# Retention followed by a bilinear FFN: slots 8 to 11 as one tile, two pairs of blocks by seven products, and a new order of all steps

## The chip, the cores and the metric

One core of one Trainium2 chip. The metric is device time in microseconds of one execution of the whole kernel. Five engines work side by side, each through its own queue in order: TensorE (PE, with its weight loads shown as PEld), VectorE (DVE), ScalarE (ACT), GpSimd (POOL) and SyncE (SP), which here issues nearly all DMAs. An instruction that waits holds up everything behind it on its engine.

## The reference

```python
# q, k, v: (4, 8, 768, 64); gamma_h = 1 - 2**(-5-h); scale = 1/8
for t in range(768):
    state = gamma * state + outer(k[t], v[t])          # per batch and head
    y[t] = scale * (q[t] @ state)
x = y.transpose(0, 2, 1, 3).reshape(3072, 512)
out = ((x @ w_a) * (x @ w_b)) @ w_out                  # w_a, w_b: 512x1536, w_out: 1536x512
```

Inputs and output are float32. The kernel computes in bfloat16 products with float32 sums.

## The kernel before

**Slots and tiles.** The 3072 tokens are 24 slots of 128, six to a batch. Attention works on slots; the FFN works on tiles of several slots: `TILES = [4, 2, 2, 2, 2, 4, 8]`. Slots 0 to 5 (three pairs, `PAIRS = 3`) come first and have routines of their own (`casts2`, `flip2`, `scores2`, ...), because their transposes are done on TensorE; from slot 6 on `flip` does them by DMA.

**A slot of attention** from slot 6 on: `scaled` multiplies k and q by tables of the decay and casts to bfloat16 into `kqb`; the cast of v goes into `vb`; `flip` transposes `kqb` into `kqT` by a DMA on SP; `update` (U) adds the slot's k, v products to the state and copies the state to SBUF; `scores` (S) gives masked scores `aT` (two products with the mask on VectorE); `inter` (I) and `intra` (N) sum the output in two PSUM banks; `leave` (L), once for two slots, copies the output to the tile `xt` on ScalarE. `turn(new, old)` does U and S of one pair of slots and I, N and L of the pair before it in one go, some 70 small TensorE products without an FFN product between.

**The FFN of a tile.** The width of 1536 is 12 blocks of 128. For a block, `ffn_a` multiplies a weight block with the whole tile (four products over the depth of 512), and ScalarE casts the result to bfloat16 (`asb`); `ffn_g` does the same with the other weights and VectorE multiplies the two into `ht`. A tile of two slots has products of 256 columns, one of four slots 512. PSUM banks of these blocks come from a ring of three (`psff`).

**Seven products for eight.** A 2x2 block product can be done with seven products of sums of blocks. The kernel does this in three places: in `Group` (the output product of two slots: sums `hs` of `ht`, sums T1 to T4 of w_out; steps numbered 1, 7, 2, 6, 5, 3, 4), in `Unit` (the input products of the last tile, slots 16 to 23; sums of weights `ws` and of inputs `XS`), and in `Quad` (two pairs of blocks, 0 with 6 and 1 with 7, of the tile of slots 12 to 15, one object for each weight, sums of inputs `XF`). Results are evicted between the steps: a bank `A` keeps summing and ScalarE takes snapshots of it, which VectorE adds to the banks `B` and `C`.

**The order** of the instructions on every engine is the order of the calls in the program (`seq` pins it). It is written out by hand: for slots 6 to 15 by calls such as these, for slots 12 to 15 and the end by strings (`LACED`, `START`, `END`).

```python
blocks(3, 9, 10)
turn(12, 10)
blocks(3, 10, NFT)
hsums(3, 3, 6, G_)
casts(16)
single(3, Y0, AT0, FF)     # Group of tile 3, with blocks 0 to 2 of tile 4 between its steps
```

Weight sums for the last tiles are made on GpSimd by `weight_pieces`, a few at a time. Loads of a slot follow the `flip` of the slot two before it. `store` issues the finished output rows.

**The start.** SP issues k, q, v of pair 0, of pair 1, then the first weights. For the first six slots k, q and v come with two tokens to a partition: runs of 512 bytes.

```python
f = raw_tile([P, H, 2, D], F32, nm + "f", nm + "f")
s = src[b, :, 2 * u * P : 2 * (u + 1) * P, :].rearrange("h (p two) d -> p h two d", two=2)
seq(nc.sync.dma_start(out=f, in_=s))
```

**Buffers that matter here**: output rows `osb` have six buffers, used in turn, also for the sums `XF`; `asb` five; raw k and q two, each for two slots; `kqT` three, each for two slots; `xt` and `ht` two.

Of the kernel before, what the change touches and what calls it, by code (L numbers as in the profile page):

```python
# [9 lines left out]
F32 = mybir.dt.float32  # L10
# [5 lines left out]
TILES = [4, 2, 2, 2, 2, 4, 8]  # L16
PAIRS = 3


START = ("A1 A2 u0.1 u1.1 A6 T X3 A7 B1 X2 A5 B6 B7 X1 A3 B5 u0.2 u1.2 B2 X4 A4 u0.6 B3 u1.6 B4 u0.5 u1.5 "  # L20
         "u0.7 u2.1 u0.3 u1.7 u2.6 u1.3 u0.4 u2.2 u3.1 u2.5 u1.4 u2.7 u3.6")
END = ("u11.1 u10.5 u10.7 u9.4 u11.6 u10.3 u11.2 S03 a1< u11.5 u11.7 u10.4 b1< u11.3 a1> b1> c1< d1< u11.4 a7 c1> d1> c2 d2 "
       "S02 S01 b7 a2 b2 S04 a6 b6 S13 a5 b5 S12 a3 b3 a4 b4 S11 c7 d7 c6 d6 S14 c5 d5 "
       "c3 c4 d4 d3")
V_LATE = range(12, 20)
LACED = ("X3 X2 m1 m7 m2 a1 b1 a2 b2 m6 X1 a6 b6 a7 b7 F2 X4 m5 a5 b5 K20 G2 a3 b3 a4 b4 V18 "
         "m3 c1 d1 F3 H3 c2 d2 c6 d6 c7 d7 c5 d5 m4 c3 d3 V19 c4 d4 G3")
# [4 lines left out]
def kernel(  # L32
# [78 lines left out]

    def raw_tile(shape, dtype, tag, name):
        return raw.tile(shape, dtype, tag=tag, name=name, bufs=3 if tag == "vf" else 2)
# [3 lines left out]
    def load_slot(t, names="kqv"):  # L117
        b, ci = divmod(t, NCH)
        for nm in names:
            src = {"k": k, "q": q, "v": v}[nm]  # L120
            if nm == "q":
                if t % 2 == 0:
                    load_two(nm, src, b, ci // 2, t)
                continue
            if t % 2 == 0:
                whole[nm] = raw_tile([P, 2, H, D], F32, nm + "f", nm + "f")
            raws[nm, t] = whole[nm][:, t % 2]
            s = src[b, :, ci * P : (ci + 1) * P, :].rearrange("h p d -> p h d")
            seq(nc.sync.dma_start(out=raws[nm, t], in_=s))

    def load_slots(t):
        for u, names in ((t, "kq"), (t + 1, "k"), (t, "v"), (t + 1, "v")):
            load_slot(u, names)
# [8 lines left out]
    def load_pair(u):  # L142
        for nm, src in (("k", k), ("q", q), ("v", v)):
            load_two(nm, src, 0, u, 2 * u)
# [25 lines left out]
    def issue_loads(n):  # L170
        for _ in range(min(n, len(pending))):
            what = pending.pop(0)
            n = int(what[1:])
            if what[0] in "ab":
                load_wide(what[0], n)
            elif what[0] in "kqv":
                load_two(what[0], {"k": k, "q": q, "v": v}[what[0]], 0, n, 2 * n)
            else:
                {"p": load_pair, "s": load_slots, "t": load_slot, "w": load_w, "o": load_o}[what[0]](n)


    kqb = {}
# [11 lines left out]
    tabs = []  # L194

    def tables(pattern, channel):
# [8 lines left out]
        if not tabs:  # L205
            qtab = const.tile([P, NCH, H, 1], F32, name="qtab")
            seq(nc.scalar.activation(qtab[:, :, :, 0], earg, AF.Exp, bias=bq))
            tabs.append(qtab)
        tabs.append(ktab)

    tables([[2 * P, PAIRS], [1, 2], [0, 1]], 2)
    make_identity(nc, ident)
# [4 lines left out]
    for par in range(2):  # L217
        m = const.tile([P, 1, P], BF16, name=f"mask{par}")
        seq(nc.gpsimd.memset(m, 1.0))
        for c in range(2):  # L220
            mc = m[64 * c : 64 * c + 64]
            seq(nc.gpsimd.affine_select(out=mc, in_=mc, compare_op=ALU.is_ge, fill=0.0,
                                        base=-par, pattern=[[0, 1], [1, 2], [2, 64]],
# [5 lines left out]
    def late_tables():  # L229
# [3 lines left out]
        tables([[P, NCH], [0, 1]], 1)  # L233

# [32 lines left out]
    def cast_o(j):  # L267
        cast(nc.gpsimd, wo_bf[:, j * FPO : (j + 1) * FPO, :], wst["o", j])
# [12 lines left out]
    def scaled(eng, t, i):  # L281
        tab = tabs[0] if i else tabs[1 if t < 2 * PAIRS else 2]
# [5 lines left out]
        else:  # L288
            dst = dst.rearrange("p hp r d -> p r hp d")
# [3 lines left out]

    def new_nat(t):
        kqb[t] = nat.tile([P, 2, HP, 2, D], BF16, tag="kqb", name="kqb")
        kb[t], qb[t] = kqb[t][:, 0], kqb[t][:, 1]
        vb[t] = nat.tile([P, H, D], BF16, tag="vb", name="vb")

    def casts(t, between=lambda: None):
        new_nat(t)  # L300
        scaled(nc.gpsimd, t, 0)
        between()
        scaled(nc.gpsimd, t, 1)
        if t not in range(12, 20):
            cast(nc.gpsimd, vb[t], raws["v", t])
        u = t + 2
        if u == 20:
            load_slot(u, "kq")
        flip(t)
        if u == 20:  # L310
            load_slot(u + 1, "k")
            return
        if u == 21:
            load_slot(u - 1, "v")
            load_slot(u, "v")
            load_slot(22, "kq")
            return
        if u in V_LATE:
            if u == 13:
                load_slot(12, "q")  # L320
            elif u == 19:
                load_slot(18, "kq")
            load_slot(u, {12: "k", 18: ""}.get(u, "kq"))
            if u % 2:
                load_slot(u - 1, "v")
                load_slot(u, "v")
        elif u < NSLOT:
            load_slot(u)

    def flip(t):  # L330
        if t % 2 == 0:
# [4 lines left out]

    def late_kq(t):
        for u in (t, t + 1):
            new_nat(u)
            scaled(nc.gpsimd, u, 0)  # L340
            scaled(nc.gpsimd, u, 1)
            flip(u)
        if t == 20:
            load_slot(23, "k")
            load_slot(22, "v")
            load_slot(23, "v")

    def casts_two(t):
        for u in (t, t + 1):
            new_nat(u)  # L350
            scaled(nc.gpsimd, u, 0)
            scaled(nc.gpsimd, u, 1)
            flip(u)
        for u in (t, t + 1):
            cast(nc.gpsimd, vb[u], raws["v", u])
        load_slot(t + 3)
# [9 lines left out]
    def scores(t, where, cuts=2):  # L366
        at = score_banks(where)
# [13 lines left out]
    def update(t, eng):  # L381
        ci = t % NCH
        if ci == NCH - 1:
            return
# [17 lines left out]

    def inter(t):
        if t % NCH == 0:
            return
        for j in range(2):
# [8 lines left out]
    def intra(t):  # L415
        for r in range(2):
# [7 lines left out]
    def leave(t):  # L424
        J, i = where[t]
# [7 lines left out]

    def turn(new, old, eng=nc.scalar):
        if old is not None:
            ys[old // 2] = [psat.tile([P, 2, 2, 2, P // 2], F32, tag=f"y{r}", name="y") for r in range(2)]
        two = new is not None and (new + 1) % NCH < NCH - 1
        if new is not None:
            if two or old is None:
                update(new, eng)  # L440
            cuts = 1 if new == 8 else 2
            scores(new + 1, "y" if old is None else "ff", cuts)
            scores(new, "at", cuts)
        if old is not None:
            inter(old)
            inter(old + 1)
        if two:
            update(new + 1, nc.scalar)
        elif new is not None and old is not None:
            update(new, eng)  # L450
        if old is not None:
            intra(old)
            intra(old + 1)
            leave(old)

# [24 lines left out]

    def scores2(u, par, where="at"):
# [787 lines left out]
```

## Time and profile before

| | |
|---|---|
| median of 3 runs | 218.31 us (218.28 to 218.43) |
| span of the profiled execution | 216.6 us |
| outside the span, to the median | 1.7 us |
| TensorE busy | 210.7 us, 97% |
| GpSimd, VectorE, ScalarE busy | 154.2, 147.5, 104.9 us |
| DMA | 39.68 MB, 183 GB/s over the span |

How to read the views: a row of the timeline has the start and the length in us, the engine, the line of the kernel, the operation, the tile written and the tiles read, the shape, the count, and in brackets the idle time before it with what ended it. Products of TensorE overlap, so the distance of starts, not the length, is what one costs. A row by form has after the bar the busy time in us and the mean ns of one. A row of the windows has start and end, the length, busy time and count of PE, PEld, DVE, ACT and POOL, then the granted clock, the busy share of the DMA engines and GB/s. The lines of the kernel that appear below: L568 and L580 the blocks a and g, L685 the groups' steps, L390 U, L372 S, L410 I, L420 N, L378 the masks, L431 L, L292 the scaled casts of k and q, L251 and L249 casts, L618 sums and products of two tiles.

### The profile page before, as it was taken

What the parts mean: (1) busy time and instruction counts of PE and PEld (TensorE: products, weight loads), DVE (VectorE), ACT (ScalarE), POOL (GpSimd) and SP (SyncE); (2) the same over time, 40 slices, a digit from 0 to 9 for tenths busy, and PEclk for the clock granted to TensorE, in tenths of its full rate; (3) what the DMA queues carried; (4) which work ended last, traced back from release to release, by engine and by line L of the source; (5) the groups of instructions that cost most, each with busy time, mean ns of one, the idle gap of its engine ahead of it and who ended that gap; (6) DMA issues with size and microseconds to landing.
All of it is one profiled execution on the core that took longest, in us unless ns stands there. A gap on an engine that the chain in (4) does not pass through costs nothing.

```text
span 216.6 us, 5713 instructions
## 1 busy us (share of the span) xinstructions
PE 210.7 (97%) x2252; PEld 146.1 (67%) x2252; DVE 147.5 (68%) x272; ACT 104.9 (48%) x235; POOL 154.2 (71%) x184
## 2 busy tenths in 40 slices
PE   7889999999999999999999999999999999999994
PEld 3557445587458888888888877457864444458883
DVE  3777346845984486356377978676577987688962
ACT  3256325343224444464576475657546656652331
POOL 5265876879878678969869979899986999530000
PEclk9999999999999999999999999999999999999999
DMA  5999999999999999999979999950013000000055
GB/s 162 290 320 365 387 311 360 384 268 232 221 264 227 228 231 222 158 192 269 197 169 245 222 209 234 236 127 3 5 69 125 2 0 3 2 0 0 27 194 170
DMA packets 85162, 39.68 MB, mean 183 GB/s; under 512 B 57488, under 2 KB 78864, under 8 KB 85136
## 3 DMA queue, kind: packets, MB, share of 16 engines
q1 hardware_dynamic: 84992, 39.26, 76.8%
q8 instruction: 17, 0.28, 0.5%
q14 instruction: 9, 0.07, 0.1%
q10 hardware_dynamic: 144, 0.07, 0.1%
HBM read 28.31 MB, written 6.29 MB: 160 GB/s over the span
## 4 chain that ended last, share of the span: by engine, by line
PE 91%; SPq 3%; DMA 3%; POOL 0%; issue 0%; DVE 0%
PE a L568 18%; PE g L580 18%; PE mA L685 12%; PE uA L859 10%; PE mB L685 6%; PE o L605 5%; PE uB L859 5%; SPq L138 3%; DMA wsta<-in_moe_w_a_dram 3%; PE mC L685 3%; PE at L372 2%; PE uC L859 2%; PE y L420 2%; PE st L390 2%; PE fa L949 2%; PE fb L949 1%
## 5 line engine op out<-in xcount | busy, mean ns | idle before, releaser
L582 DVE TENSOR_TENSOR ht<-g,asb 128x256 bf16<-128x256 f32 (+1 forms) x70 | 34.4, 493 | 31.6 <-PE g L580 28.0
L568 PE MATMUL a<-xt,wa_bf 128*128 128x256 bf16 (+1 forms) x280 | 48.6, 300 | 0.1
L580 PE MATMUL g<-xt,wb_bf 128*128 128x256 bf16 (+1 forms) x280 | 48.4, 300 | 0.0
L571 ACT CAST asb<-a 128x256 bf16<-128x256 f32 (+1 forms) x70 | 30.0, 429 | 33.3 <-PE a L568 31.1
L580 PEld LDWEIGHTS <-wb_bf 128*128 128x128 bf16 x280 | 27.0, 98 | 10.2 <-POOL wb_bf L251 0.2
L568 PEld LDWEIGHTS <-wa_bf 128*128 128x128 bf16 x280 | 26.5, 98 | 10.7 <-POOL wa_bf L251 0.4
L292 POOL TENSOR_TENSOR kqb<-kf,ktab 128x512 bf16<-128x512 f32 x22 | 23.6, 1078 | 7.4 <-DMA kf<-in_k_dram 4.9
L866 ACT COPY snap<-uA 128x512 f32<-128x512 f32 x36 | 20.0, 588 | 15.4 <-PE uA L859 13.9
L685 PEld LDWEIGHTS <-hs 128*128 128x128 bf16 x234 | 22.8, 98 | 3.6
L378 DVE TENSOR_TENSOR aT<-at,mask 128x512 bf16<-128x512 f32 x36 | 22.3, 682 | 0.3
L292 POOL TENSOR_TENSOR kqb<-qf,qtab 128x512 bf16<-128x512 f32 x18 | 19.6, 1088 | 2.7 <-DMA qf<-in_q_dram 2.7
L618 POOL TENSOR_TENSOR ht<-gsb,asb 128x512 bf16<-128x512 bf16 x13 | 15.2, 1175 | 7.5 <-DVE gsb L618 7.4
L692 ACT COPY snaps<-mA 128x256 f32<-128x256 f32 x30 | 11.0, 374 | 18.9 <-PE mA L685 18.9
L685 PEld LDWEIGHTS <-ht 128*128 128x128 bf16 x180 | 17.5, 98 | 3.3
L618 POOL TENSOR_TENSOR hs<-ht 128x384 bf16<-128x384 bf16 (+3 forms) x14 | 15.9, 1134 | 3.5 <-DVE ht L582 3.5
L618 POOL TENSOR_TENSOR hs<-ht,hs 128x384 bf16<-128x384 bf16 (+1 forms) x17 | 16.9, 997 | 1.5 <-DVE ht L582 1.4
L685 PE MATMUL mA<-wsum,hs 128*128 128x256 bf16 x120 | 15.2, 273 | 0.0
L618 DVE TENSOR_TENSOR osb<-mB,snaps 128x256 f32<-128x256 f32 x20 | 8.4, 421 | 8.3 <-ACT snaps L692 4.4
L251 POOL CAST vb<-vf 128x512 bf16<-128x512 f32 x12 | 7.5, 641 | 6.7 <-DMA vf<-in_v_dram 6.7
L605 PE MATMUL o<-wo_bf,ht 128*128 128x512 bf16 x48 | 10.7, 379 | 0.0
L618 DVE TENSOR_TENSOR asb<-uB,snap 128x512 bf16<-128x512 f32 x12 | 8.2, 685 | 3.1 <-ACT snap L866 2.0
L618 DVE TENSOR_TENSOR gsb<-uB,snap 128x512 bf16<-128x512 f32 x12 | 8.2, 686 | 2.9 <-ACT snap L866 2.1
(138 smaller groups left out, 374.7 us busy)
## 6 DMA issues: line engine op xcount, KB each, us to landing
qf<-in_q_dram SPq DMA_DIRECT2D x12, 512.0 KB, 6.1
out_dram<-osb SPq DMA_DIRECT2D x21, 256.0 KB, 4.1
kf<-in_k_dram SPq DMA_DIRECT2D x18, 256.0 KB, 5.1
vf<-in_v_dram SPq DMA_DIRECT2D x18, 256.0 KB, 5.3
wsta<-in_moe_w_a_dram SPq DMA_DIRECT2D x6, 512.0 KB, 7.7
wsto<-in_moe_w_out_dram SPq DMA_DIRECT2D x6, 512.0 KB, 8.7
wstb<-in_moe_w_b_dram SPq DMA_DIRECT2D x5, 512.0 KB, 8.3
kf<-in_k_dram SPq DMA_DIRECT2D x3, 512.0 KB, 7.1
```

Of the source, the lines that this page charges most:

```text
L292: seq(eng.tensor_tensor(dst, src, tab, op=ALU.mult))
L378: seq(nc.vector.tensor_tensor(aT[t][:, r], at[r], mask.to_broadcast([P, HP, P]), op=ALU.mult))
L568: seq(nc.tensor.matmul(a, wa_bf[:, kt, fs], xcols(J, kt, c0, c1), start=(kt == 0), stop=(kt == KT - 1)))
L571: seq(nc.scalar.copy(asb, a))
L580: seq(nc.tensor.matmul(g, wb_bf[:, kt, fs], xcols(J, kt, c0, c1), start=(kt == 0), stop=(kt == KT - 1)))
L582: seq(nc.vector.tensor_tensor(ht[J][:, ft, c0:c1], g, asbs.pop((J, ft, c0)), op=ALU.mult))
L605: seq(nc.tensor.matmul(o, ht[J][:, ft, i * P : (i + 1) * P], wo_bf[:, ft], start=(ft == 0), stop=(ft == NFT - 1), skip_group_check=True))
L618: seq(eng.tensor_tensor(dst, x, y, op=op))
L685: seq(nc.tensor.matmul(m, w, right[:, j], start=(first and j == 0), stop=(j == NP - 1), skip_group_check=True))
L692: seq(nc.scalar.copy(self.snaps[:, n], self.bank["A"]))
L859: seq(nc.tensor.matmul(m, w, right[:, k], start=(first and k == 0), stop=(k == 1), skip_group_check=True))
L866: seq(nc.scalar.copy(self.snaps[n], self.bank["A"]))
```

## The change

`TILES` becomes `[4, 2, 2, 4, 4, 8]`: slots 8 to 11 are one tile of four slots. `Quad` is replaced by `Duo`, which does both weights of a pair of blocks in one object; a bank holds both weights' halves of 256 columns, so that one eviction serves both. It is used for two pairs of blocks in tile 3 (slots 8 to 11) and in tile 4 (slots 12 to 15); the other eight blocks of each are plain, with 512 columns.

From the blocks of tile 1 on, one string `ORDER` of 597 steps replaces the calls of `turn`, `single`, `blocks`, `laced` and `big`. Each step is one call, with the engine where there is a choice (D VectorE, G GpSimd, A ScalarE): `a.J.ft` and `g.J.ft` blocks, `M.J.i.x` step x of a group, `d.J.p.x` step x of a Duo, `u.n.x` of a Unit, `U`, `S`, `I`, `N`, `L` of attention one slot at a time, `k`, `y` (q), `v` casts, `f` transposes, `l` loads, `s` stores, `h`, `x`, `X`, `w`, `W` sums, `C` casts of w_out. U, S, I and N of a turn may now stand apart. Some casts of k, q and v, weight sums and sums of `ht` move to another engine.

For the first three pairs q is loaded with eight tokens to a partition, in runs of 2 KB, by two DMAs of 256 KB. The table of q, the masks, the reading of the transposed q in scores and the write of the outputs follow that order of tokens; four small iotas, eight memsets, three small products and one exponential are added at the start.

```diff
-TILES = [4, 2, 2, 2, 2, 4, 8]
+TILES = [4, 2, 2, 4, 4, 8]
...
+DUO = {3: {0: ('F', 'b', 'F', 'DGG', 'KKT'), 1: ('F', 'Z', 'F', 'DGG', 'OTO')}, 4: {0: ('F', 'b', 'F', 'DGG', 'KKT'), 1: ('F', 'Z', 'F', 'DGG', 'OTO')}}
...
+ORDER = """
+a.1.0 w.a.3.0.2.G C.4.G s w.a.2.0.2.D s C.3.G a.1.1 C.0.G C.2.G s a.1.2 w.b.3.0.2.D g.1.1 s C.5.G g.1.0 s
+a.1.3 w.a.1.0.2.D a.1.7 a.1.6 s g.1.2 k.7.G g.1.6 a.1.8 g.1.7 s a.1.4 C.1.G a.1.9 a.1.10 g.1.3 s
...
+o.1.0 S.6.at.2 s S.7.y.2 v.7.G s o.1.1 h.1.3.0.6.D o.3.0 k.9.A h.1.2.0.6.D l.q.10 s v.10.G s o.3.1
+h.1.4.0.6.D v.9.G y.9.G h.1.1.0.6.D l.v.11 U.7.A l.k.11 N.6 N.7 v.8.A f.9 I.7 I.6 L.6 k.10.G M.1.0.1
+M.1.0.7 a.2.0 s y.11.G g.2.0 M.1.0.6 a.2.4 s a.2.1 M.1.0.5 a.2.2 l.v.12 y.10.A g.2.2 g.2.1 M.1.0.4 k.11.G
...
+y.12.G g.2.7 g.2.6 h.2.2.0.3.G f.12 U.9.A s N.8 l.q.14 I.8 I.9 h.2.1.0.3.G S.11.ff.2 l.k.14 U.10.A N.9
+k.13.G S.10.at.2 L.8 s a.2.9 s a.2.10 g.2.10 l.q.16 g.2.9 l.v.15 I.10 I.11 h.2.4.0.3.D N.10 N.11 L.10 s
+a.2.11 g.2.11 h.2.2.3.6.G h.2.1.3.6.G y.13.G h.2.4.3.6.G M.2.0.1 l.k.15 M.2.0.7 x.3.3.D y.14.G d.3.0.1
+x.3.2.D v.12.G d.3.0.7 x.3.1.D f.13 s M.2.0.6 d.3.0.2 M.2.0.2 d.3.0.6 d.3.1.1 a.3.2 x.3.4.D M.2.0.5
...
+M.2.0.4 U.12.A f.15 d.3.0.4 f.14 d.3.1.4 g.3.3 y.16.G v.13.A d.3.1.3 a.3.8 l.v.16 S.13.y.2 k.16.G v.14.G
+S.12.at.2 f.16 l.v.17 s a.3.9 g.3.8 h.3.3.0.4.G g.3.9 s S.14.at.2 I.12 I.13 v.15.A N.12 U.13.D N.13
...
+h.3.2.4.6.G h.3.4.4.6.D I.15 N.14 l.q.20 U.15.A N.15 h.3.1.4.6.D l.k.20 v.16.G L.14 l.v.19 f.18 M.3.0.7
+l.q.22 l.v.20 l.v.21 y.19.G M.3.0.2 M.3.0.6 k.19.G l.k.21 x.4.3.G S.17.y.2 f.19 S.16.at.2 U.16.A M.3.0.5
+l.k.22 x.4.2.D M.3.1.1 M.3.0.3 M.3.1.7 y.22.G M.3.0.4 v.17.G y.20.G d.4.0.1 M.3.1.2 l.k.23 d.4.0.2
+d.4.1.1 M.3.1.6 x.4.1.D d.4.0.6 x.4.4.D s k.20.G d.4.0.7 d.4.1.2 d.4.0.5 k.21.D f.20 M.3.1.5 d.4.1.7
+v.18.G l.v.22 a.4.2 l.v.23 y.21.G d.4.0.3 k.23.G s d.4.0.4 h.4.3.0.1.G k.22.D d.4.1.6 M.3.1.3 y.23.G
+M.3.1.4 d.4.1.5 f.21 g.4.2 d.4.1.3 a.4.3 d.4.1.4 g.4.3 h.4.3.1.2.G h.4.2.0.2.G v.19.A N.17 U.18.A
...
+"""
...
+    def load_pair_q(u):
+        f = raw_tile([P, 2, 8 * D], F32, "qf", "qf")
+        s = q[0, :, 2 * u * P : 2 * (u + 1) * P, :].rearrange("(hp r) (n j) d -> r hp n (j d)", r=2, j=8)
+        for r in range(2):
+            seq(nc.sync.dma_start(out=f[:, r], in_=s[r]))
+        raws["q", 2 * u] = raws["q", 2 * u + 1] = f
...
+    def queries2(u, rows, hp, c):
+        at = 32 * hp + 16 * c
+        return kqT2[u][rows, :, 1, :, at : at + 16]
...
-    class Quad:
+    class Duo:
...
+        def product(self, bank, left, right, first):
...
+            for n, w_ in enumerate("ab"):
+                m = self.bank[bank][:, n * DH : (n + 1) * DH]
...
         def leave(self, i, c, bank, n):
...
+            ab = asbp.tile([P, 4 * P], BF16, tag="asb", name="ab")
+            tt(ab, self.bank[bank], self.snaps[n], ALU.add)
...
+            tt(ht[self.J][:, ft, c * DH : (c + 1) * DH], ab[:, :DH], ab[:, DH:], ALU.mult, self.engines["CBA".index(bank)
+               if bank == "C" else 1 + int(n == 1)])
```

678 lines of the change are left out of this document (296 added, 382 removed).

## The prediction

> **What bounds the kernel now.** I read the page first, then the windows by stage, then the timeline of TensorE at the places that the change touches.
>
> ```profile
> span 216.6 us, 5713 instructions
> ...
> PE 210.7 (97%) x2252; PEld 146.1 (67%) x2252; DVE 147.5 (68%) x272; ACT 104.9 (48%) x235; POOL 154.2 (71%) x184
> ```
>
> ```profile
> 16.00:42.00 26.00, 25.91 (x279) 14.48 (x272) 15.99 (x26) 11.44 (x23) 18.82 (x28) 1.00 1.08 359
> 64.00:116.00 52.00, 51.99 (x687) 45.05 (x686) 29.82 (x63) 27.24 (x69) 41.45 (x47) 1.00 1.15 213
> 116.00:152.00 36.00, 35.98 (x516) 24.68 (x515) 27.81 (x52) 22.33 (x52) 33.41 (x37) 1.00 0.87 177
> 152.00:213.00 61.00, 61.00 (x415) 38.93 (x410) 47.48 (x76) 30.57 (x63) 34.24 (x34) 1.00 0.12 42
> ```
>
> The columns are busy time of TensorE, its weight loads, VectorE, ScalarE, GpSimd, then clock, DMA share and GB/s. From 16 us to 213 us TensorE is never idle at full clock. So the end moves only by TensorE's own work, by the moment at which its dense stream begins, and by waits that the new order adds; a gap can only be added, there is almost none to remove. GpSimd (33.41 of 36) and VectorE (27.81 of 36) are close behind in the stage of slots 12 to 23. The sum is made against the profiled execution: span 216.6, and 1.7 outside it to the median of 218.31, which I leave as it is.
>
> **Products: 1.0 us removed.** A block of four products is priced by the distance of starts.
>
> ```profile
> 44.80 0.60 PE L568 MATMUL a<-xt,wa_bf 128*128 128x256 bf16 x4
> ...
> 51.78 0.60 PE L568 MATMUL a<-xt,wa_bf 128*128 128x256 bf16 x4
> ...
> 135.61 1.03 PE L580 MATMUL g<-xt,wb_bf 128*128 128x512 bf16 x4
> 136.47 1.03 PE L568 MATMUL a<-xt,wa_bf 128*128 128x512 bf16 x4
> 137.34 1.03 PE L580 MATMUL g<-xt,wb_bf 128*128 128x512 bf16 x4
> ```
>
> ```profile
> 65.93 0.66 PE mB L685 x6
> ```
>
> Sixteen short blocks lie between the first two rows: 6.98 / 16 = 0.436 us, 0.109 a product. A long block is (137.34 - 135.61) / 2 = 0.865. Slots 8 to 11 now take 48 short blocks (12 blocks, two weights, two tiles): 20.9 us. After, 8 blocks stay plain, 16 long ones, 13.8; the two pairs take 2 x 7 steps, each of four 256-wide products (two weights, two halves of the depth), 14 x 0.436 = 6.1. Together 19.9, so -1.0. Slots 12 to 15 have that form already, in 28 steps of two products; they only change their grouping: 0. Output groups and the last tile keep their products.
>
> **Attention cut into more visits: +0.8 us.** One turn of before, on TensorE:
>
> ```profile
> 95.97 0.60 PE L580 MATMUL g<-xt,wb_bf 128*128 128x256 bf16 x4
> 96.50 0.32 PE L390 MATMUL st<-vb,kqb 128*64 128x64 bf16 x8
> 96.74 0.64 PE L372 MATMUL at<-kqT 64*64 64x128 bf16 x32
> 97.22 0.39 PE L410 MATMUL y<-kqT,gst 64*64 64x128 bf16 x16
> 97.54 0.32 PE L390 MATMUL st<-vb,kqb 128*64 128x64 bf16 x8
> 97.69 0.62 PE L420 MATMUL y<-aT,vb 128*64 128x128 bf16 x16
> 98.23 0.61 PE L568 MATMUL a<-xt,wa_bf 128*128 128x256 bf16 x4
> ```
>
> The block at 95.97 should end its stream at 96.41, the state products start at 96.50: 0.09 to go from the 128*128 form to another. The same eight state products take 0.24 when a 64*64 form follows and 0.15 when 128*64 follows: 0.09 again. I counted such changes in both orders, for slots 6 to 23: before 39, in 11 visits (a turn is one visit); the new order spreads the steps U, S, I and N over 16 visits with 48 changes. 9 x 0.09 = +0.8. Ends: 0.4, if some hide behind the last product's stream, to 1.2.
>
> **Start: -0.45 us.**
>
> ```profile
> 5.04 1.29 DVE L292 TENSOR_TENSOR kqb<-kf,ktab 128x512 bf16<-128x512 f32 x2 [0.84 <-DMA kf<-in_k_dram]
> 10.52 2.04 POOL L292 TENSOR_TENSOR kqb<-kf,ktab 128x512 bf16<-128x512 f32 x2 [0.71 <-DMA kf<-in_k_dram]
> 15.52 1.18 POOL L251 CAST wa_bf<-wsta 128x512 bf16<-128x512 f32 x2 [0.33 <-DMA wsta<-in_moe_w_a_dram]
> 16.19 1.17 PE L568 MATMUL a<-xt,wa_bf 128*128 128x256 bf16 x8
> ```
>
> ```profile
> 7.00:12.00 5.00, 4.56 (x76) 2.84 (x78) 4.33 (x8) 1.81 (x4) 2.65 (x4) 1.00 1.22 290
> 21.00:27.00 6.00, 6.00 (x32) 2.93 (x30) 2.23 (x4) 2.08 (x5) 4.72 (x8) 1.00 1.05 387
> ```
>
> Here everything waits for loads, which run at 290 GB/s in 512-byte runs; the wide weight pieces, in 2 KB runs, get 387. 512 KB of q then take 1.36 us for 1.81, 0.45 less. One q stands ahead of the second pair's keys (10.52), two ahead of the first weights (15.52). The chain to the first dense product (16.19) runs over the keys of pair 1, their casts, transposes and scores, so it moves by one of them, 0.45; the weights, 0.9 earlier, cease to limit. Ends 0 and 0.9. [...]
> Paid there: four small iotas on GpSimd, eight memsets and three products of 48 columns on VectorE, one more exponential on ScalarE. VectorE idles 0.84 before 5.04 and GpSimd 0.71 before 10.52, which covers them; without that cover they cost their own few tenths. Scores of the first pairs read queries in runs of 16 instead of 64, which no row shows. The nearest row has 32 score products in 0.48 (96.74 to 97.22); at half pace the two pairs in the chain would lose 1.0, a gain has no reason. I take 0, since the count of products and columns stays.
>
> **New waits: +1.6 us.** From slot 6 on every queue has a new order, and TensorE issues in order. I went along it for places where the step ahead on another engine is longer than TensorE's work meanwhile.
>
> ```profile
> 60.63 0.59 ACT L249 COPY osb<-o 128x512 f32<-128x512 f32 x1 [2.00 <-PE o L605]
> 61.71 0.37 ACT L249 CAST gst<-st 128x256 bf16<-128x256 f32 x1 [0.50 <-PE st L390]
> ...
> 65.10 1.07 ACT L431 CAST xt<-y 128x512 bf16<-128x512 f32 x2
> ```
>
> ```profile
> L249 ACT CAST vb<-vf 128x512 bf16<-128x512 f32 x12 | 7.5, 621 | 0.0
> ```
>
> a.2.0, first block of tile 2: ScalarE has the output copy of o.3.1, U.7, v.8 and then L.6 in its queue: 0.59 + 0.37 + 0.62 + 1.07 = 2.65. TensorE has U, two N and one I (1.0 with three changes) and two steps of six (1.31): 2.3. Wait 0.35 and a hand-over: 0.4 (0.2 to 0.6).
>
> ```profile
> 97.21 2.48 DVE L378 TENSOR_TENSOR aT<-at,mask 128x512 bf16<-128x512 f32 x4
> ```
>
> ```profile
> L582 DVE TENSOR_TENSOR ht<-g,asb 128x256 bf16<-128x256 f32 x52 | 22.1, 425 | 20.6 <-PE g L580 17.1 <-ACT asb L571 2.5 <-POOL hs L618 0.5
> L618 DVE TENSOR_TENSOR xf<-xt 128x512 bf16<-128x512 bf16 x2 | 1.9, 946 | 0.0
> L618 DVE TENSOR_TENSOR hs<-ht 128x512 bf16<-128x512 bf16 x1 | 0.6, 644 | 0.0
> ```
>
> d.3.0.7 needs x.3.3: after N.11 come L.10 (1.07), the cast of a.2.11 (0.37, like the one of the same shape at 61.71), the product of g.2.11 (0.42) and the sum (0.95): 2.8, and four hand-overs between engines; TensorE has 0.09 + 0.87 + 1.31 + 0.44 = 2.7. Wait 0.3 (0.1 to 0.6).
> a.1.7 needs the bank of g.1.1, whose product on VectorE stands behind two weight sums (0.64 to 0.95 each). TensorE has six short blocks, 2.6; VectorE some 2.65 to 3.3, tile 0's last product included: 0.2 (0 to 0.6).
> S.11 takes two banks of the ring of three just after S.9, S.8 and three blocks: four masks 2.48 and two products 0.85 against 3.4 on TensorE: 0.1.
>
> ```profile
> 104.00:107.00 3.00, 3.00 (x30) 2.70 (x28) 1.27 (x3) 1.43 (x5) 2.40 (x4) 1.00 1.33 224
> ```
>
> ```profile
> DMA to landing us min/median/max: 3.1/4.7/6.4
> ```
>
> S.14 waits for the transposes of slot 14, queued on SP behind slot 15's and so behind GpSimd's y.15; landing takes 3.1 to 6.4 (the row of the transposes), TensorE has three long blocks after S.12: 0.2 (0 to 1.5).
> The dearest place: M.3.1.5 takes the output tile that M.3.0.2 filled, six tiles earlier in a ring of six. Its store is queued on SP after l.q.20 to l.k.23: 2 x 0.52 + 10 x 0.26 MB with itself, 3.7 MB, at 224 GB/s 16.4 us. TensorE has 11.7 us of work from U.15, beside that load in the order, to M.3.1.5, and SP may be 1.5 us ahead of it; VectorE then stands for about 3.2 us. Behind it are queued six instructions (some 4 us with its own) before the bank of g.4.2 is free for g.4.3; TensorE has 7.0 us of other steps until there, 3 us of cover. Wait 0.4 (0 to 1.8).
> Together 0.4 + 0.3 + 0.2 + 0.1 + 0.2 + 0.4 = 1.6. What goes: small waits of under 0.12 each at the short blocks of slots 8 to 11, -0.2.
>
> Sum: -1.0 + 0.8 - 0.45 + 1.6 - 0.2 = about +0.8. Span 217.4, time **219.1 us**.
>
> **Rivals.** *The side engines keep up* (other side). The waits come from means of single instructions; back to back these run closer, four masks in 2.48 where the mean of one gives more. If each of the four or five instructions ahead of a wait is 0.06 to 0.1 shorter, or starts before TensorE's last product ends, the waits at a.2.0, d.3.0.7 and a.1.7 close; the point is 0.3 us per place, and stores that land within 3 us of M.3.1.5. Against it: ScalarE's queue at a.2.0 holds nothing that can go earlier. It gives 218.3 - 1.0 + 0.8 - 0.45 - 0.2 = 217.5. Half of the waits gives 218.3, no change.
> *The stores are late.* Same place, the loads held by GpSimd or going at 200 GB/s: 18.3 us for 3.7 MB, 2 us more of wait: 221.0. For: DMA is full until 116 us. Against: GpSimd may let SP be further ahead.
> *The 2 KB runs bring nothing*, because keys and values alone set the start: 219.1 + 0.45 = 219.6. [...]
>
> **Numbers.** A run can tell about 0.2%, 0.44 us, from no change: 217.87 to 218.75. Chances: forecast with its waits 0.40, stores late 0.14, 2 KB runs nothing 0.06, all three slower: 0.60. Half the waits, no change: 0.15. Side engines keep up: 0.25. The range reaches down past 217.5 to 217.2, with a start of 0.7 instead of 0.45, and up to 221.0. The likeliest case's own range is 218.75 to 219.9.
>
> **What would show it.** Right: fewer 256-wide rows for tile inputs, 512-wide from slots 8 on; the first dense block at about 15.75; gaps on TensorE before a.2.0, d.3.0.7 and at the blocks after M.3.1.5, where VectorE's output row waits for a store; 16 visits. Wrong: TensorE without gaps from 16 us to its end, or a gap of over 1 us at another place, such as a load that arrives late at GpSimd.

## The result: 18.6 us slower

| | before | after |
|---|---|---|
| median | 218.28 us (218.20 to 218.43, 5 runs) | 236.91 us (235.47 to 237.23, 5 runs) |
| profiled execution, span | 216.6 us | 233.8 us (time 235.47) |
| ratio | | 1.0843, interval 1.0816 to 1.0870 |

The forecast was 219.1, with a range of 217.2 to 221.0. The size was wrong by a factor of over twenty. The sign was right, in part by luck: most of the loss is in the step that the forecast had put down as a gain. One execution of q_alone_by_head, a kernel of the experiments below, took 755.31 us in a slow state and is left out of its time.

The page of the profile after: span, TensorE's busy time, the granted clock, the DMA engines and the chain that ended last.

```profile
span 233.8 us, 5522 instructions
...
PE 218.5 (93%) x2163; PEld 142.8 (61%) x2180; DVE 158.9 (68%) x292; ACT 108.9 (47%) x248; POOL 131.3 (56%) x159
...
PEclk9955699979999999999999999999999999999999
DMA  4877998799899999989899999980002100000044
...
PE 69%; DMA 14%; SPq 6%; DVE 4%; issue 3%; ACT 2%; POOL 1%; ACTq 0%; DVEq 0%; POOLq 0%
```

TensorE's share of the span falls from 97% to 93%. 14% of the chain that ended last is DMA, where the kernel before has 3%. In the slices from about 12 to 29 us the granted clock is 0.5 to 0.6 of full speed. The windows, with the columns as in the prediction:

```profile
7.00:12.00 5.00, 0.79 (x8) 0.59 (x5) 0.20 (x1) 1.01 (x1) 0.00 (x0) 0.88 0.72 166
16.00:42.00 26.00, 25.64 (x253) 15.30 (x251) 11.76 (x22) 10.41 (x22) 15.95 (x24) 0.77 0.92 285
64.00:116.00 52.00, 51.68 (x584) 37.48 (x586) 36.93 (x68) 30.15 (x84) 33.86 (x37) 1.00 1.08 218
116.00:152.00 36.00, 33.51 (x422) 22.82 (x426) 29.22 (x49) 15.72 (x34) 23.57 (x25) 1.00 1.15 226
```

In the first of them all engines stand: TensorE has 0.79 us of work in 5 (before 4.56), and the loads run at 166 GB/s with a share of 0.72, where the kernel before had 290 and 1.22. Behind that idle stretch the granted clock is low: 0.77 on the mean from 16 to 42 us, where the kernel before had 1.00. TensorE idles 2.5 us between 116 and 152 us (0.02 before), a stretch in which the new order waits, as shown below. The start by rows of the timeline (L369 is the scaled cast of the first pairs' q, L210 its DMAs):

```profile
5.16 1.28 DVE L387 TENSOR_TENSOR kqb<-kf,ktab 128x512 bf16<-128x512 f32 x2
6.87 5.48 SPq L210 DMA_DIRECT2D qf<-in_q_dram  x2
11.79 1.29 DVE L369 TENSOR_TENSOR kqb<-qf,qtab 128x512 bf16<-128x512 f32 x2 [5.35 <-DMA qf<-in_q_dram]
21.91 1.29 DVE L369 TENSOR_TENSOR kqb<-qf,qtab 128x512 bf16<-128x512 f32 x2 [4.09 <-DMA qf<-in_q_dram]
26.18 1.83 PE L624 MATMUL a<-xt,wa_bf 128*128 128x256 bf16 x8
46.57 1.29 DVE L369 TENSOR_TENSOR kqb<-qf,qtab 128x512 bf16<-128x512 f32 x2 [3.17 <-DMA qf<-in_q_dram]
```

The same places in the kernel before, and the first block of tile 1, before and after:

```profile
6.84 1.29 DVE L292 TENSOR_TENSOR kqb<-qf,qtab 128x512 bf16<-128x512 f32 x2 [0.51 <-DMA qf<-in_q_dram]
12.21 1.50 DVE L292 TENSOR_TENSOR kqb<-qf,qtab 128x512 bf16<-128x512 f32 x2 [0.17 <-DMA qf<-in_q_dram]
42.06 0.61 PE L568 MATMUL a<-xt,wa_bf 128*128 128x256 bf16 x4
```
```profile
56.34 0.83 PE L624 MATMUL a<-xt,wa_bf 128*128 128x256 bf16 x6
```

The keys of pair 0 are there as before (5.16 against 5.04), but its q comes at 11.79 instead of 6.84, that of pair 1 at 21.91 instead of 12.21. SP needs 5.48 us to issue q of pair 1 and holds the values and weights behind it. The first dense block stands at 26.18 instead of 16.19, and after pair 2's q, which is late as well, the first block of tile 1 starts at 56.34 instead of 42.06: 14.3 us.

### The profile page after: what moved, and what is told of

It is laid out like the page before. It is cut to its first block, busy times and chain, and to the rows that moved or that the text cites. A ratio compares the mean times of both kernels' runs of the same rounds, so it can differ in the third digit from the quotient of the medians.

```text
span 233.8 us, 5522 instructions
## 1 busy us (share of the span) xinstructions
PE 218.5 (93%) x2163; PEld 142.8 (61%) x2180; DVE 158.9 (68%) x292; ACT 108.9 (47%) x248; POOL 131.3 (56%) x159
## 4 chain that ended last, share of the span: by engine, by line
PE 69%; DMA 14%; SPq 6%; DVE 4%; issue 3%; ACT 2%; POOL 1%; ACTq 0%; DVEq 0%; POOLq 0%
DMA qf<-in_q_dram 12%; PE a L624 11%; PE g L637 10%; PE mA L738 9%; PE uA L888 9%; PE mB L738 5%; PE o L660 4%; PE uB L888 4%; SPq L210 3%; PE mC L738 2%; PE uC L888 2%; SPq L198 2%; PE fA L987 2%; PE at L429 2%; DMA out_dram<-osb 2%
## 5 line engine op out<-in xcount | busy, mean ns | idle before, releaser
L639 DVE TENSOR_TENSOR ht<-g,asb 128x256 bf16<-128x256 f32 (+1 forms) x54 | 29.0, 551 | 21.8 <-PE g L637 18.9
L624 PE MATMUL a<-xt,wa_bf 128*128 128x256 bf16 (+1 forms) x211 | 42.2, 332 | 0.3
L637 PE MATMUL g<-xt,wb_bf 128*128 128x256 bf16 (+1 forms) x212 | 40.3, 325 | 0.2
L637 PEld LDWEIGHTS <-wb_bf 128*128 128x128 bf16 x216 | 20.9, 98 | 12.7 <-issue 0.7
L624 PEld LDWEIGHTS <-wa_bf 128*128 128x128 bf16 x216 | 20.7, 100 | 12.5 <-issue 0.7
L895 ACT COPY snap<-uA 128x512 f32<-128x512 f32 x36 | 20.2, 590 | 14.5 <-PE uA L888 14.3
L387 POOL TENSOR_TENSOR kqb<-kf,ktab 128x512 bf16<-128x512 f32 x17 | 18.6, 1097 | 9.5 <-ACT vb L329 4.0
L676 POOL TENSOR_TENSOR hs<-ht,hs 128x512 bf16<-128x512 bf16 (+1 forms) x9 | 9.9, 1101 | 8.8 <-DVE hs L676 7.9
L527 PE MATMUL tp<-ident,kqb 128*128 128x128 bf16 x48 | 5.9, 279 | 7.4 <-DVE kqb L369 7.0
L369 DVE TENSOR_TENSOR kqb<-qf,qtab 128x512 bf16<-128x512 f32 x6 | 3.9, 688 | 12.6 <-DMA qf<-in_q_dram 12.6
L504 ACT CAST xt<-y 128x512 bf16<-128x512 f32 x18 | 9.7, 594 | 4.4 <-PE y L491 4.4
L331 POOL CAST wb_bf<-wstb 128x512 bf16<-128x512 f32 (+2 forms) x11 | 6.9, 653 | 7.9 <-DMA wstb<-in_moe_w_b_dram 7.9
```

The costliest lines, as they stand in the source:

```text
L331: seq(engine.tensor_copy(dst, src))
L387: seq(eng.tensor_tensor(dst, src, tab, op=ALU.mult))
L624: seq(nc.tensor.matmul(a, wa_bf[:, kt, fs], xcols(J, kt, c0, c1), start=(kt == 0), stop=(kt == KT - 1)))
L637: seq(nc.tensor.matmul(g, wb_bf[:, kt, fs], xcols(J, kt, c0, c1), start=(kt == 0), stop=(kt == KT - 1)))
L639: seq(nc.vector.tensor_tensor(ht[J][:, ft, c0:c1], g, asbs.pop((J, ft, c0)), op=ALU.mult))
L676: seq(eng.tensor_tensor(dst, x, y, op=op))
```

## Experiments on the start

**q_alone**: the kernel before with only the new q.

> Kernel before with only the change of the first pairs' q (two DMAs of 256 KB in 2 KB runs, new table, masks, reading of queries, output rows). It measures the start alone. Theory of the spread: first dense block at about 26 us instead of 16.2, tile 1 about 14 us later, 218.3 + 14 = 232 to 233. Rival, the start's delay is mostly taken up later where the order of before has slack: under 229. The forecast's step, 0.45 us faster, would be 217.9.

Measured 232.47 us, ratio 1.0652 (1.0628 to 1.0677): +14.2. The first dense block is at 26.50. This one part by itself costs as much as three quarters of the loss.

**q_two**: the same, each DMA cut once more.

```diff
         for r in range(2):
-            seq(nc.sync.dma_start(out=f[:, r], in_=s[r]))
+            for i in range(2):
+                seq(nc.sync.dma_start(out=f[64 * i : 64 * i + 64, r], in_=s[r, 2 * i : 2 * i + 2]))
```

> The kernel before with the new q layout, each of the two DMAs to a pair cut once more, so that the outermost dimension is 2 instead of 4. Theory of the spread (engines reached = outermost dimension, the same ones for each DMA): two engines do all of it, 512 KB of a pair take about 13 us instead of 6.5, first dense block at 38 to 42 us instead of 26, time 245 to 250. Rival (two DMAs in flight use different engines): as q_alone, 232. Rival (the number of engines doesn't count, the layout does): 232.

Measured 247.27 us, ratio 1.1326 (1.1307 to 1.1345); q of pair 0 reaches VectorE at 17.18, the first dense block starts at 36.37. A window in which only q was on its way, of q_two, and one of the kernel after:

```profile
21.00:22.00 1.00, 1.00 (x13) 0.78 (x9) 1.00 (x3) 0.00 (x0) 1.00 (x2) 0.50 0.13 49
```
```profile
10.20:10.80 0.60, 0.00 (x0) 0.00 (x0) 0.00 (x0) 0.00 (x0) 0.00 (x0) 0.96 0.34 76
```

The second to last column is the mean share of 16 engines: 0.13 is two of them, at 49 GB/s. In the kernel after 0.34 is between five and six: four, and the tail of other loads. Counted from the packets' records up to 24 us, exactly four packets of 2 KB are in flight for 9.4 us in the kernel after, and exactly two for 14.2 us in q_two; the wide weight pieces mostly have 16. So such a DMA reached as many engines as the outermost dimension of its source is long: 4 pairs of heads, or 2.

**by_head**: the kernel after, four DMAs to a pair, each with 32 tokens outermost; **q_alone_by_head** and **q_alone_heads** (one kernel, measured twice): the same in the kernel before.

```diff
+        s = q[0, :, 2 * u * P : 2 * (u + 1) * P, :].rearrange("(hp r) (n j) d -> hp n r (j d)", r=2, j=8)
+        for hp in range(HP):
+            seq(nc.sync.dma_start(out=f[32 * hp : 32 * hp + 32], in_=s[hp]))
```

> Kernel after, only the loads of the first pairs' q changed: four DMAs of 128 KB to a pair, one for each pair of heads, so that the outermost dimension of each is 32 tokens instead of 4 pairs of heads; runs of 2 KB, layout, tables, masks and order as they were. Theory of the spread (a DMA reaches only as many of the 16 engines as its outermost dimension is long; q's has 4): the loads of the start run at 290 to 390 GB/s, the first dense block returns from 26.2 us to 15.7 to 16.5, TensorE's dense stream of tile 1 from 56.3 to about 42, and the time falls by about 14 us, from 236.9 to 221 to 223. Rival, the layout itself is slow (2 KB written to single partitions, or the new order of tokens): the first dense block stays near 26 us and the time at 235 to 237. Rival, the number of DMAs: eight or four small ones cost more on SP than two, the time rises above 237.

> Kernel before with the change of the first pairs' q, loaded by four DMAs to a pair, one for each pair of heads. Theory of the spread with the forecast's price for 2 KB runs (387 instead of 290 GB/s): first dense block at 15.7 us, time 217.8; with no gain from 2 KB runs and some tenths for SP's two more issues to a pair: 218.3 to 218.9. Rival, the layout itself is slow: 232.

> The same kernel as q_alone_by_head (kernel before, q of the first pairs by four DMAs to a pair), for a profile of its start. In by_head, with the new order, q of pair 0 reached VectorE at 7.70 instead of 6.84 and q of pair 1 at 13.81 instead of 12.21: 1.6 us; the 2 KB packets took 145 ns each against 88 ns for those of the wide weight pieces. Theory (all 16 engines write the same 32 partitions at a time, and this is slow): the same here, first dense block at 17.8 to 18.2, and 1.6 to 2 us of the 4.9 come from the start; the rest from the third pair's q, whose loads stand between the weights. Rival (something else than the start, in the order after it): first dense block by 16.6.

Measured 226.52 us (ratio 1.0392, 1.0342 to 1.0443), and 222.99 and 221.88 (1.0208, 1.0179 to 1.0237; 1.0174, 1.0157 to 1.0191); the first two are slower than the 221 to 223 and 217.8 to 218.9 that were expected. The first dense block is back from 26.50 to 18.48 in q_alone_heads, not to 16: the number of engines was most of it, but 3.6 to 4.7 us stay. A window of by_head in which q is loaded:

```profile
11.00:12.00 1.00, 1.00 (x31) 0.83 (x24) 0.76 (x2) 0.00 (x0) 0.50 (x1) 0.64 1.06 224
```

All engines are busy (1.06) and bring 224 GB/s. The 2 KB packets took some 145 ns each; those of the wide weight pieces 88.

**q_quarters**: the kernel before with its old 512-byte runs, q cut into four DMAs of 32 partitions.

```diff
-        seq(nc.sync.dma_start(out=f, in_=s))
+        for i in range(4):
+            c = slice(32 * i, 32 * i + 32)
+            seq(nc.sync.dma_start(out=f[c], in_=s[c]))
```

> The kernel before with its old q layout (512-byte runs), the load of each of the first pairs' q cut into four DMAs of 32 partitions each. Theory (16 engines that write the same 32 partitions at a time are slow, as the 145 ns for 2 KB in by_head suggested): the 512-byte packets of q take 45 to 60 ns instead of 34, q of pair 1 reaches VectorE about 1.0 to 1.5 us later, 219.5 to 221. Rival (the 2 KB runs or the order of tokens are slow, not the 32 partitions): 34 ns, and at most 0.5 us for SP's six more issues: 218.3 to 218.8.

Measured 224.13 us, ratio 1.0308 (1.0244 to 1.0371), more than expected. While q is loaded, the 512-byte packets took 42 to 54 ns where the kernel before has 34. So the slowness of by_head comes with writing 32 partitions at a time, and neither the longer runs nor the order of tokens are needed for it. That four small DMAs are slow in themselves was not tested apart: no run has four that each write all 128 partitions. The two DMAs to a pair of q_interleaved below do write all 128, and their 2 KB packets took 91 to 107 ns, against 133 to 151 in by_head. In q_quarters q and the loads behind it come late, TensorE stands 0.86 us up to 8.85, the granted clock is 0.5 from 9 to 18 us, and the first dense block is at 21.16. How much of the 5.8 us is the load and how much the half clock was not separated.

**q_contiguous** and **setup_alone** measure two sizes of the forecast by themselves. q_contiguous loads other tokens' data, in runs of 4 KB: it keeps the bytes and leaves out the arrangement of tokens and heads.

```diff
 q_contiguous:
-            s = src[b, :, 2 * u * P : 2 * (u + 1) * P, :].rearrange("h (p two) d -> p h two d", two=2)
+            s = src[b].rearrange("h s d -> (h s d)")[2 * u * P * DM : 2 * (u + 1) * P * DM]
 setup_alone:
+    for h in range(H):
+        seq(nc.vector.memset(lgp[32 * (h // 2) : 32 * (h // 2) + 32, :, h % 2], lg[h]))
...
+    seq(nc.scalar.activation(qtab2[:, :, :, :, 0], argq, AF.Exp, bias=bq))
```

> The kernel before, the first pairs' q read as contiguous memory, 4 KB to a partition, by one DMA to a pair that writes all 128 partitions (other tokens' data; nothing else changed). It prices the forecast's step by itself: 512 KB of q at 387 instead of 290 GB/s, -0.45 to -0.9: 217.4 to 217.9. Rival (2 KB and longer runs bring nothing at the start, since 512-byte runs are at the rate of the memory or keys and values set the start): 218.2 to 218.4.

> The kernel before with the set-up instructions of the new q layout alone (eight memsets, four iotas, three products, one exponential, whose results are not used) and the old loads. The forecast put them at nothing, covered by VectorE's idle 0.84 us before the first cast. Theory now: in by_head the first cast of keys began at 5.42, with the new order's set-up, instead of 5.04, so the cover was 0.4 us short: 218.7. Rival (covered further on): 218.3.

Measured 217.83 us (ratio 0.9979, 0.9971 to 0.9988) and 218.28 (0.9999, 0.9990 to 1.0008). Long runs that all 16 engines write to all 128 partitions do gain 0.46 us, and beside the old loads the set-up is covered. The first dense block of q_contiguous and its window:

```profile
15.72 1.05 PE L573 MATMUL a<-xt,wa_bf 128*128 128x256 bf16 x8
```
```profile
7.00:12.00 5.00, 4.77 (x85) 3.13 (x83) 4.33 (x9) 2.11 (x4) 3.02 (x4) 1.00 1.15 321
```

15.72 is what the forecast had (15.75), and 321 GB/s stand against the 290 of before.

**q_interleaved** and **after_interleaved**: q with the partition as 4n + hp, in the kernel before and in the kernel after.

```diff
-        s = ....rearrange("(hp r) (n j) d -> r hp n (j d)", r=2, j=8)
+        s = ....rearrange("(hp r) (n j) d -> r n hp (j d)", r=2, j=8)
...
+    for i in range(HP):
+        seq(nc.scalar.dma_start(out=qtab2[i::HP], in_=qtabh[32 * i : 32 * i + 32]))
...
-        return kqT2[u][rows, :, 1, :, at : at + 16]
+        return kqT2[u][rows, :, 1, :, 64 * c + hp : 64 * c + 64 : HP]
```

> The kernel before with q of the first pairs in 2 KB runs, but with the partition as 4 times the group of eight tokens plus the pair of heads, so that the outermost dimension of each of the two DMAs to a pair is 32 and 16 engines write 128 partitions; the table is turned into that order by four small DMAs, and the scores read queries four columns apart. Theory (the loss was the order of dimensions alone; q_contiguous gained 0.46): 217.8 to 218.0. Rival (set-up through four more DMAs, 128 pieces of 192 bytes, delays the first q beyond its load, or queries read four columns apart are slower): 218.3 to 219.5.

> The kernel after with the same repair of q's load. If the account is right (18.6 = 14.2 for q's loads and the rest for the order, which with the loads of before cost 6.5): the old q with the new order, 224.8, less the 0.46 of longer runs: 224.3, between 223.3 and 225.5. Rival (an earlier start closes or moves waits of the new order): under 222.5 or over 226.

Measured 233.6 and 234.68 us (1.0680, 1.0649 to 1.0711; 1.0761, 1.0719 to 1.0803), far from what was expected. A window and two rows of q_interleaved:

```profile
7.00:12.00 5.00, 0.39 (x5) 0.20 (x2) 0.00 (x0) 0.88 (x3) 2.44 (x4) 0.68 1.15 319
```
```profile
5.04 6.04 ACTq L232 DMA_DIRECT2D qtab<-qtabh  x4
15.72 1.87 DVE L311 TENSOR_TENSOR kqb<-qf,qtab 128x512 bf16<-128x512 f32 x2 [9.28 <-DMA qtab<-qtabh]
```

The load itself is repaired: 319 GB/s, as in q_contiguous. But VectorE waits 9.28 us for the table, whose four small DMAs took ScalarE 6.04 us to issue and landed at 15.7, beside full loads from SP (share 1.15). The rival, set-up that delays the first q, holds, at a size it had not named. Its other half, queries read four columns apart, does not: 32 score products take 1.10 us at 19.14, and 1.07 in the kernel after at 14.64, both at a granted clock of 0.5. So a correct kernel with the 0.46 us was not shown; it needs the table without a DMA, which was not tried. after_interleaved does not close the account for the same reason; it is 1.1 us above q_interleaved.

## Experiments on the order

**old_q**: the kernel after with the q of before (loads, table, masks, scores and output rows of the first pairs undone; tiles, Duo and string kept).

> Kernel after with q of the first pairs loaded and laid out as in the kernel before (512-byte runs, one table, the old masks and output rows); tiles, Duo and the new order stay. It measures the new order alone. Theory that the q loads cost about 14.3 us of the 18.6 and the order the rest: 221 to 223. The forecast's sum without its term for the start (products -1.0, form changes +0.8, waits +1.6, small waits -0.2) would be 218.3 + 1.2 = 219.5. Rival, the order costs most because its waits add up in a row behind late loads: over 225.

Measured 224.80 us, ratio 1.0305 (1.0248 to 1.0362): +6.5, where the forecast without its start had +1.2. The four executions lie between 223.60 and 226.53 us. Rows of TensorE, GpSimd and a window of old_q (L402 scores, L311 the cast of v, L360 the casts of k and q, L705 the groups' steps):

```profile
67.57 1.18 POOL L311 CAST vb<-vf 128x512 bf16<-128x512 f32 x2 [9.74 <-DMA vf<-in_v_dram]
...
81.35 0.42 PE L402 MATMUL at<-kqT 64*64 64x128 bf16 x16 [1.46 <-DMA kqT<-kqb]
...
117.25 1.39 POOL L360 TENSOR_TENSOR kqb<-qf,qtab 128x512 bf16<-128x512 f32 x1 [7.59 <-DMA qf<-in_q_dram]
...
120.80 0.39 PE L705 MATMUL mA<-wsum,hs 128*128 128x256 bf16 x2 [0.91 <-POOL hs L643]
```
```profile
82.00:84.00 2.00, 2.00 (x33) 1.37 (x28) 2.00 (x4) 1.61 (x4) 2.00 (x2) 0.57 0.87 207
```

GpSimd stands 9.74 us for the load of v.10 and 7.59 us for that of q.18. Behind the second wait is a sum of `ht` (h.3.2.4.6), and TensorE waits for that sum; before S.11, at 81.35, TensorE waits for the transposes of slot 11. After that wait the granted clock is 0.57 for 4 us; by an estimate from these two numbers that costs 4 x 0.43 = 1.7 in this execution. It has a mean clock of 0.992 over the span; at 1.000 and 0.997 the kernel took 223.60 and 224.05 us, so with little of such stretches the order costs 5.3 to 5.8 us. The distances of TensorE's starts beyond the products' own columns give 5.5 us of gaps over 0.12 each more than in the kernel before.

**sum_first**, **loads_first**, **both_first**, **gp_order** move these places in the string of old_q (written out from the strings, with the steps between left out):

```diff
 sum_first:   -y.18.G a.3.10 a.3.11 g.3.10 k.18.G g.3.11 ... h.3.2.4.6.G
              +a.3.10 a.3.11 g.3.10 g.3.11 ... h.3.2.4.6.G y.18.G k.18.G
 loads_first: -l.k.10 W.2.D y.8.G f.8 ... l.v.10 ... l.q.10 s v.10.G s ... v.9.G y.9.G h.1.1.0.6.D l.v.11 U.7.A l.k.11
              +l.k.10 l.v.10 l.q.10 l.k.11 l.v.11 W.2.D y.8.G f.8 ... s s ... v.9.G y.9.G h.1.1.0.6.D v.10.G U.7.A
 both_first:  both, and l.q.18 l.k.18 right behind l.v.17
 gp_order:    sum_first, v.10.G behind y.9.G, and k.13.G y.13.G behind the sums h.2.x.3.6
```

> The kernel with the old q and the new order (224.8 us), with one exchange on GpSimd's queue: the sum h.3.2.4.6 stands ahead of y.18 and k.18 instead of behind them. In the trace of the old q GpSimd stood 7.6 us at y.18 for q's load, which SP had issued at 111.05 behind two stores; the sum, and with it TensorE at 119.6, 120.9 and 122.9 (1.08 + 0.44 + 0.70 of gaps), waited behind it. Theory (a load late at GpSimd holds what is queued behind it): these gaps go, 224.8 - 2.2 = 222.6. Rival (the wait is handed on, since slot 18's transposes then come later and the scores S.18 and S.19 wait): 224 to 225. Rival (the gaps are the sums' own time on the side engines): no change, 224.8.

> The kernel with the old q and the new order (224.8 us), with the loads of v.10, q.10, k.11 and v.11 moved on SP's queue ahead of the transposes of slot 8 and of the stores behind which they stood, and GpSimd's cast v.10 behind y.9. In the trace of the old q GpSimd stood 9.7 us at v.10 for its load, and TensorE 1.63 us at 79.7 for the transposes of slot 11, after which the granted clock was 0.57 for 4 us (1.7 us lost). Theory (place of the loads in the queue): both go, 224.8 - 3.3 = 221.5. Rival (the DMA engines are full in that stretch, share 0.8 to 1.8, so the loads land no earlier or others land later): 224 to 225. Half, the gap goes short but the loads behind come later: 222.5 to 223.5.

> Both of these edits, and the loads of q.18 and k.18 ahead of the two stores behind which they stood. Theory (the order's cost is loads and transposes that come late at GpSimd and TensorE, not products or changes of form): 224.8 - 2.2 - 3.3 = 219.3, and 0.2 to 0.7 less where the forecast's -1.0 of products shows. Rival (new waits take the place of the old): 221.5 or more.

> The kernel with the old q and the new order (224.8 us), GpSimd's queue alone changed in three places: the cast v.10 behind y.9, the casts k.13 and y.13 behind the sums h.2.x.3.6, y.18 and k.18 behind h.3.2.4.6; SP's queue, and so the loads, as they were. Theory (GpSimd, held by a late load, holds TensorE's sums): the gaps of hs at 119 us and those at 86 to 89 us go, 221 to 222.5. Rival (the loads are late in any case and the transposes behind them hold TensorE instead): 223.5 to 225.

Measured 224.0, 224.97, 225.27 and 225.69 us (ratios 1.0260, 1.0242 to 1.0278; 1.0293, 1.0273 to 1.0313; 1.0313, 1.0299 to 1.0327; 1.0329, 1.0303 to 1.0354). None of them can be told apart from old_q's 223.60 to 226.53. The gaps that were named went or shrank (S.11: 1.63 to 0.31 in loads_first; the three gaps behind the sum: 2.2 to 1.3 in sum_first), but others grew: 1.98 us at x.3.3 in sum_first; 1.13 and 1.24 there and at tile 2's group in loads_first; 2.18 before S.14 in gp_order. In sum_first GpSimd now stood for the sum's own input, with y.18, k.18 and v.16 behind it:

```profile
115.07 1.46 POOL L643 TENSOR_TENSOR hs<-ht,hs 128x512 bf16<-128x512 bf16 x1 [7.54 <-DVE ht L608]
```

The rival, that waits are handed on, holds all four times in the traces; in time gp_order lies above its range of 223.5 to 225. None of the places that were moved carries the loss by itself.

**fast_loads**, **fast_loads_before**, **fast_sum_first**: loads of slots 6 to 23 as contiguous memory, in old_q, in the kernel before, and in old_q with the sum and the loads of slot 18 moved. Like q_contiguous they load other tokens' data.

```diff
-            s = src[b, :, ci * P : (ci + 1) * P, :].rearrange("h p d -> p h d")
+            s = src[b].rearrange("h s d -> (h s d)")[ci * P * DM : (ci + 1) * P * DM]
```

> The kernel with the old q and the new order (224.8 us), with k, q and v of slots 6 to 23 read as contiguous memory: the same bytes, buffers and queues, but runs of 2 to 4 KB to a partition instead of 256 and 512 bytes, so that each load is done in some 0.7 us of the DMA engines instead of about 1.2. It leaves out the right arrangement of tokens and heads (the loaded data are other tokens'). Theory (the order's cost is loads that land late because the DMA engines are full until 141 us; the last loads land at 140.4, 140.8 and 141.4 in three orders): the gaps of 5.4 us and the half clock behind them go, 218.3 to 219.5. Rival (the queues of GpSimd, VectorE and ScalarE and the transposes in their new order, whatever the loads do): 222 or more.

> The kernel before with the same faster loads (also with other tokens' data). Control: TensorE has no gap after 16 us, so 218.3 within 0.5, if the loads are hidden there. If it gains over 1 us, the loads limit the old order too and fast_loads has to be read against it.

> The kernel fast_loads (220.7 us; other tokens' data) with the sum h.3.2.4.6 ahead of y.18 and k.18 on GpSimd and the loads of q.18 and k.18 ahead of the two stores. In fast_loads the gaps that are left after 52 us are 0.72 + 0.43 + 0.70 = 1.85, all at the steps that wait for this sum. Theory (hold of GpSimd by a load): they go, 218.8, within 0.3 of fast_loads_before (218.9), so that the order itself costs nothing: products -0.85 and changes of form together about +0 against before. Rival (the wait is handed on as in sum_first, which gained 0.8 of 2.2): 220 or more.

Measured 220.66, 218.92 and 220.27 us (ratios 1.0106, 1.0091 to 1.0121; 1.0030, 1.0019 to 1.0042; 1.0091, 1.0077 to 1.0105). Windows of old_q, then of fast_loads:

```profile
64.00:80.00 16.00, 15.53 (x203) 12.99 (x202) 8.35 (x19) 10.33 (x30) 5.98 (x7) 1.00 1.12 230
80.00:100.00 20.00, 18.52 (x202) 14.14 (x202) 13.16 (x22) 9.80 (x21) 15.58 (x16) 0.91 1.04 219
100.00:130.00 30.00, 27.77 (x345) 17.75 (x343) 23.42 (x41) 12.09 (x26) 18.58 (x19) 1.00 1.04 214
```
```profile
64.00:80.00 16.00, 16.00 (x212) 13.32 (x214) 11.54 (x20) 10.89 (x33) 10.28 (x9) 1.00 0.82 212
80.00:100.00 20.00, 20.00 (x234) 15.38 (x228) 16.06 (x27) 10.88 (x24) 14.99 (x17) 1.00 0.71 212
100.00:130.00 30.00, 28.64 (x352) 19.14 (x351) 24.23 (x43) 13.01 (x27) 19.31 (x20) 1.00 1.07 248
```

With the same bytes in fewer, longer packets the DMA share falls to 0.82 and 0.71, TensorE works 16.00 of 16 and 20.00 of 20, and the clock is whole. Against its control, fast_loads_before, the new order then costs 1.7 us instead of 6.5: some 4.8 of the 6.5 are there only with the slower loads, and the half clock of old_q went with them. The control lost 0.6, so the old order was not held by its loads. What is left in fast_loads is mostly the gaps behind the sum h.3.2.4.6 (1.85 us); fast_sum_first gained only 0.4 of them, since v.16, which stands behind the sum on GpSimd, was late then (1.2 us before U.16). Whether a string can be found in which nothing waits stays open.

## Why the prediction was wrong, point by point

**Products, -1.0: right.** Blocks a in the kernel after:

```profile
L624 PE MATMUL a<-xt,wa_bf 128*128 128x512 bf16 x99 | 26.2, 388 | 0.3
L624 PE MATMUL a<-xt,wa_bf 128*128 128x256 bf16 x112 | 16.0, 283 | 0.0
```

Before there were 72 and 208. (By the program 104 products are of 512 columns, as old_q's trace has them; five records are missing here.) From the starts: from the first block of tile 1 to TensorE's last product sum_first takes 5.1 us longer than the kernel before, of which 5.3 are gaps over 0.12 us and 0.6 smaller ones; the columns give -0.85.

**Forms, +0.8: right within its ends.** The same count of small distances gives +0.6 in sum_first and +0.9 in fast_loads, inside the ends of 0.4 and 1.2.

**Start, -0.45: the step that failed.** It measured +14.2. "512 KB of q then take 1.36 us for 1.81" took the rate of the wide weight pieces, 387 GB/s, for a DMA of another shape. What longer runs are worth was priced rightly (-0.46 measured in runs of 4 KB, first dense block at 15.72; in runs of 2 KB the loads of q_interleaved reached 319 GB/s against 321, but no kernel gives them a time of their own), the cover of the set-up rightly (218.28), and scores that read in runs of 16 are as fast as before: 32 products take 0.64 in by_head at 17.15 and 0.64 in the kernel before at 15.21. In place of a load at 387 GB/s the runs showed one on 4 of 16 engines (four packets in flight for 9.4 us), 166 GB/s from 7 to 12 us, with SP's queue held behind it (5.48 us to issue q of pair 1). What the step never asked is over how many engines the DMA is laid and which partitions it writes at a time. The row to look for is not a rate but a shape: every load in the trace of before has 128 partitions outermost, so the bound of 0.9 from rows of that trace could not hold for one with 4. In the runs the number of engines goes with the source: with 4 outermost four packets were in flight, with 2 two (share 0.13), and with 32 the share was 1.06 (by_head) and 1.15 (q_interleaved), all 16 engines. No run shows why. Nor does one show why 32 partitions at a time are slower: the 2 KB packets took 133 to 151 ns in by_head, and 91 to 107 in q_interleaved, which writes all 128.

**New waits, +1.6: mis-sized too, since the mechanism was too narrow.** With the forms and the products, the order was to cost 1.2 and measured 6.5 with the old q. In the kernel after there is no gap over 0.12 us at a.2.0, d.3.0.7, a.1.7 or S.11, which had 1.0 together. S.14 has 0.38 (0.2). The store behind the loads is there, about as forecast in place and size: 0.6 to 0.75 us (0.4). But what stands for it is a snapshot that ScalarE takes for the second Duo of tile 4, which needs one of the six output buffers (the last row below), not VectorE's row. Pieces of the chain that ended last in the kernel after:

```profile
120.98 5.38 DMA qf<-in_q_dram
...
126.52 0.73 POOL kqb L387
...
129.01 1.12 POOL hs L676
...
142.80 3.89 DMA out_dram<-osb
...
146.78 0.59 ACT snapf L1000
```

The first three rows are a wait that the forecast did not see: the load of q.18, issued behind two stores, then GpSimd's cast, then the sum, then TensorE (0.40 + 0.57 + 0.66 us between 129.7 and 133). The steps were costed by the durations of the engines, with the loads of q, k and v taken as landed when their first reader comes to them. The forecast named a load late at GpSimd among what would prove it wrong, but gave it no price. It had the row that warned of it: a DMA share of 1.15 from 64 to 116 us.

**The account.** 14.2 for q and 6.5 for the order make 20.7, not 18.6. On top of the late start the order costs only 4.4 (236.91 - 232.47). SP's last load of v is issued 10.3 us later in the kernel after than in old_q (146.3 against 136.0), while TensorE is 14.3 us late, so the loads are nearer to being on time; that is argued from these times, not tested.

**Rivals.** "The 2 KB runs bring nothing" had the right place and no idea of the size. "Stores are late" exists at 0.6 to 0.75 us. "The side engines keep up" is nearly true of the places that it named, and the time is 19 us away from it all the same.

## What to carry to other kernels

Price a changed load by its shape, not by the length of its runs: look at the outermost dimension of its source (here 4 reached four engines, 2 two, 32 all 16 by the share) and at the partitions that it writes at a time (2 KB packets took 133 to 151 ns with 32, 91 to 107 with 128), and take the rate from a row whose load has the same shape. When an order is rewritten in a stage where the DMA share is over 1 (1.04 to 1.12 in old_q from 64 to 130 us), cost each load as a step of the chain, with its place in the issuing queue and what stands on the engine behind its first reader. Where moving one step removes a gap and the time stays, the resource behind all the gaps is the thing to measure.

## What the runs showed that was not expected

- DMAs of 256 KB with 4 outermost ran on 4 engines (four packets in flight). The six of them cost 14.2 us in all, with SP's queue standing behind them as well (5.48 us to issue two) and the granted clock at 0.5 from 12 to 26 us, behind the stretch in which TensorE idled.
- 16 engines writing the same 32 partitions brought 224 GB/s (by_head, share 1.06); packets of 512 B took 42 to 54 ns instead of 34 (q_quarters), of 2 KB about 145 instead of 88 (by_head).
- Four DMAs with 32 pieces of 192 B each, issued from ScalarE beside full loads of SP (share 1.15), took 6.04 us to issue and landed some 11 us after the first was begun. Why so long stays open.
